# A mixture-of-streams attention block on one Trainium2 core: V computed batch by batch, with batch 1's input loaded among the V weights

## The chip, the cores and the metric

The kernel runs on one core of one Trainium2 chip. Time is device microseconds (us) of a run; a kernel's figure is the median of its runs. The profile is one execution, and its span is about 1.8 us shorter than the time of that run (119.9 of 121.67 for the kernel before). Each run carries the mean granted clock of TensorE, as a share of full speed. PE is TensorE and PEld its weight loads, DVE is VectorE, ACT is ScalarE, POOL is GpSimd; PSUM is the memory that takes PE's results. An evacuation is the copy of a finished sum out of PSUM by DVE or ACT. LN is layer norm.

## The reference, cut to what matters

There are two batches of 256 image tokens and 32 text tokens, width D = 1152, in bf16. The part at stake is the image side, up to the start of Q:

```python
mod_i = (_silu(c) @ wmod_img).reshape(B, 6, 1, D)        # shift, scale, gate
hi = _layernorm(x_img, axis=-1) * (1 + sci) + shi
qkvi = hi @ wqkv_img                                      # q, k, v
# ... the same for text; joint attention over 288 tokens; out_i = x_img + gai * (ai @ wo_img)
```

The kernel splits V: (LN(x)·(1+scale)) @ Wv comes first and needs no shift; the shift's share, one row per batch, is added later. So V can start when x and the scale weights are there, before the shift weights arrive.

## The kernel before

All weights come over one DMA queue in the order in which they are issued. These are the first loads (KT = 9 row groups of 128 rows, so V has 9 row groups of weights):

```python
for b in range(B):
    nc.sync.dma_start(x_i[:, b * TPB:(b + 1) * TPB, :], ...)        # both batches of x
SCC = (0, 3, 5, 7, K8, KT)
for r0, r1 in zip(SCC, SCC[1:]):
    nc.sync.dma_start(w_sc_i[:, r0:r1, :], sc_v[:, r0:r1, :])       # scale weights
for r0, r1 in ((0, 1), (1, 3), (3, 6), (6, KT)):
    nc.sync.dma_start(w_v_i[:, r0:r1, :], v_v[:, r0:r1, :])         # V weights
w_sh_i = load_w(2, wmod_img, 0)                                     # shift, then Q, K, ...
```

PE does every matmul and transpose in program order (`mm` and `tr` pin each instruction behind the one written before it; `pin` does so on DVE and ACT). PSUM is split into a main pool of six banks (`ps_mm`) and a small pool of two (`ps_tr`); a new tile takes a free bank of its pool or waits until one is released. Transposed x goes from PSUM to `xT_i`, and a DVE instruction scales it into `hS_i`, the operand of V that PE's weight loads take (PEld lines read `hS_i`).

```python
sc_cols(0, 3); warm_up(3); sc_cols(3, 5); warm_up(1); sc_cols(5, 7)   # (one line each)
x_transposes(0, 1)()                    # batch 1's transposes among the scale columns
out31 = x_transposes(3, 1)
sc_cols(7, K8); sc_cols(K8, KT)
out61 = x_transposes(6, 1)
out61()
# ... scale + 1, x_scale of both batches ...
v_open(A0, 0, 3)                        # A0: four tiles of batch 0, 512 wide
v_open(A1, 0, 3)                        # A1: two tiles of batch 1
v_open(A0 + A1, 3, KT - 2)
v_open(A0 + A1, KT - 2, KT, kt_major=False)
p_sh = mod_rows_of(w_sh_i, sT32)        # shift rows: need the shift weights
sh_i = mod_cols_of(p_sh, "shc")
v_open([(2, 1)], 0, 4)
# ... shift, the rest of V, the shift's share of V ...
qk_img(w_q_i, 0, ...)                   # the img Q block
```

## Time and profile before

The time is 121.91 us (121.82 to 122.08, 3 runs). The first lines of the page give the span and each engine's busy time:

```profile
span 119.9 us, 2608 instructions
PE 113.7 (95%) x1121; PEld 67.1 (56%) x1121; DVE 55.9 (47%) x146; ACT 34.4 (29%) x73; POOL 11.1 (9%) x28
```

PE is busy 95% of the span. This is the whole list of the view of waits on PE (who waited for whom: us in total, times, longest):

```profile
PE wps L61 <- DVE warm L121: 1.2, 1, 1.2
PE tp L64 <- DVE xn_i L187: 0.6, 1, 0.6
PE gps L61 <- DMA t<-in_wmod_img_dram: 0.5, 1, 0.5
PE vps L61 <- DVE hS_i L220: 0.3, 1, 0.3
```

Here `wps` are warm-up matmuls, `tp` transposes of x, `vps` sums of V, `gps` a pass that multiplies rows by the shift weights. The timeline of PE (start, length, instruction, idle before it) shows the stretch that the change touches:

```profile
14.24 11.90 PE L61 MATMUL vps<-t,hS_i 128*128 128x512 bf16 x54 [0.31 <-DVE hS_i L220]
26.61 1.29 PE L61 MATMUL gps<-t,sT 128*32 128x288 bf16 x36 [0.47 <-DMA t<-in_wmod_img_dram]
27.83 6.07 PE L61 MATMUL vps<-t,hS_i 128*128 128x512 bf16 x54
33.83 1.29 PE L61 MATMUL gps<-t,shT 128*32 128x288 bf16 x36
35.05 11.83 PE L61 MATMUL ps<-xT_i,t 128*128 128x512 bf16 x54
```

V starts at 14.24, PE waits 0.47 us for the shift weights at 26.61, and Q starts at 35.05. From 26.61 PE has no gap until the last output tile. So the start of Q, 35.05, is the number to watch: what moves it moves the end.

The trace also records when each transfer's sixteen parts have landed. The last part counts, because PE waits for the whole transfer:

| landed at, us | kernel before |
|---|---|
| V row groups 3 to 5 | 18.08 |
| shift weights | 26.57 |
| Q weights | 33.48 |

With 54 matmuls in 11.90 us (six per row group, about 1.3 us), PE reaches row group 3 at about 18.1, just as its rows land. The Q weights land at 33.5, so no reordering can start Q before that.

### The profile page before, as it was taken

To read this page: it belongs to the slowest core of one execution; us is meant where nothing else is said; L and a number is where in the kernel's file an instruction comes from. 1 tells how busy PE (TensorE), PEld (TensorE's weight loads), DVE (VectorE), ACT (ScalarE), POOL (GpSimd) and SP (SyncE) were. 2 spreads that over 40 slices of the span, in tenths; PEclk is the share of its full clock that TensorE was granted. 3 is DMA by queue.
4 is the path that set the end of the run, shared out by engine and by line. 5 is a ranking of instruction groups with operands and counts; after the bars stand their busy time and mean duration, and the time that the engine had idled before them with its cause. 6 is when DMAs were issued, how large, how long until landed. Compare 5 with 4: busy or idle time off the path is not lost.

```text
span 119.9 us, 2608 instructions
## 1 busy us (share of the span) xinstructions
PE 113.7 (95%) x1121; PEld 67.1 (56%) x1121; DVE 55.9 (47%) x146; ACT 34.4 (29%) x73; POOL 11.1 (9%) x28
## 2 busy tenths in 40 slices
PE   5989899989999999999999999999999999999980
PEld 2338744445664444544448448386777766567660
DVE  1568690066837222131721203037785756666670
ACT  4799700055713104101011111125348610000000
POOL 7410000000000000000000000000222708100000
PEclk9999999999999999999999999999999999999999
DMA  4999999999999999999999999999999991420222
GB/s 118 375 408 406 402 404 414 410 414 410 406 369 416 401 412 412 413 411 412 405 412 412 415 401 413 413 404 411 413 399 408 414 357 52 143 98 0 104 76 72
DMA packets 18502, 40.88 MB, mean 341 GB/s; under 512 B 907, under 2 KB 1435, under 8 KB 18491
## 3 DMA queue, kind: packets, MB, share of 16 engines
q1 hardware_dynamic: 17616, 39.56, 84.7%
q0 software_dynamic: 480, 0.89, 2.2%
q10 hardware_dynamic: 395, 0.26, 0.7%
q8 instruction: 9, 0.15, 0.4%
q14 instruction: 2, 0.02, 0.0%
HBM read 39.38 MB, written 1.34 MB: 340 GB/s over the span
## 4 chain that ended last, share of the span: by engine, by line
PE 74%; DMA 20%; SPq 1%; DVE 1%; issue 0%
PE ps L61 52%; DMA t<-in_wmod_img_dram 20%; PE gps L61 6%; PE aps L61 6%; PE vps L61 5%; PE sps L61 4%; PE pT_ps L64 1%; SPq L97 1%; DVE tmp L565 1%; DVE o L566 0%; SPq L101 0%; PE tpt L64 0%
## 5 line engine op out<-in xcount | busy, mean ns | idle before, releaser
L61 PE MATMUL ps<-xT_i,t 128*128 128x512 bf16 x162 | 36.0, 379 | 0.0
L61 PEld LDWEIGHTS <-t 128*128 128x128 bf16 x405 | 22.7, 97 | 19.3 <-issue 0.7
L61 PE MATMUL ps<-t,aT 128*128 128x384 bf16 (+3 forms) x153 | 20.2, 308 | 0.0
L61 PE MATMUL vps<-t,hS_i 128*128 128x512 bf16 (+1 forms) x108 | 18.0, 326 | 0.3 <-DVE hS_i L220 0.3
L61 PEld LDWEIGHTS <-aT 128*128 128x128 bf16 (+1 forms) x153 | 13.0, 101 | 7.1 <-issue 0.5
L61 PEld LDWEIGHTS <-hS_i 128*128 128x128 bf16 x108 | 9.0, 98 | 9.0 <-DVE hS_i L220 0.5
L155 DVE CAST qkT<-ps 128x512 bf16<-128x512 f32 (+1 forms) x6 | 3.8, 636 | 15.4 <-PE ps L61 15.4
L435 POOL DMA_DIRECT2D mod_scratch<-g_sb x4 | 2.5, 636 | 79.7 <-ACT g_sb L157 79.7
L565 DVE TENSOR_TENSOR tmp<-ps,gb 128x384 bf16<-128x384 f32 (+2 forms) x13 | 6.8, 527 | 6.3 <-PE ps L61 6.3
L61 PE MATMUL wps<-warm 128*128 128x512 bf16 x27 | 8.2, 454 | 1.2 <-DVE warm L121 1.2
L333 DVE TENSOR_SCALAR qkT<-ps 128x512 bf16<-128x512 f32 (+1 forms) x5 | 3.3, 665 | 10.8 <-PE ps L61 10.8
L335 ACT ACTIVATE qkT<-ps 128x512 bf16<-128x512 f32 (+1 forms) x6 | 3.3, 553 | 15.5 <-PE ps L61 15.5
L157 ACT CAST qkT<-ps 128x512 bf16<-128x512 f32 (+1 forms) x5 | 2.8, 565 | 16.6 <-PE ps L61 16.6
L155 DVE CAST v_i<-vps 128x512 bf16<-128x512 f32 x5 | 3.4, 689 | 8.0 <-PE vps L61 8.0
L61 PE MATMUL gps<-t,sT 128*32 128x288 bf16 x180 | 6.4, 287 | 0.5 <-DMA t<-in_wmod_img_dram 0.5
L61 PE MATMUL aps<-pT,v_i 128*128 128x288 bf16 x36 | 6.7, 287 | 0.0
L61 PEld LDWEIGHTS <-sT 128*32 128x32 bf16 x180 | 4.5, 96 | 2.4 <-issue 2.0
L537 DVE TENSOR_SCALAR aT<-aps,svc 128x288 bf16<-128x288 f32 x9 | 4.7, 518 | 2.4 <-PE aps L61 2.3
L61 PE MATMUL sps<-qkT 128*128 128x288 bf16 (+1 forms) x54 | 5.5, 287 | 0.0
L157 ACT CAST v_i<-vps 128x512 bf16<-128x512 f32 x4 | 2.3, 586 | 10.6 <-PE vps L61 10.6
L61 PEld LDWEIGHTS <-warm 128*128 128x128 bf16 x27 | 2.7, 110 | 4.6 <-issue 1.7
L539 ACT ACTIVATE aT<-aps,svc 128x288 bf16<-128x288 f32 x9 | 4.5, 501 | 2.5 <-PE aps L61 2.5
(94 smaller groups left out, 105.1 us busy)
## 6 DMA issues: line engine op xcount, KB each, us to landing
t<-in_wmod_txt_dram SPq DMA_DIRECT2D x3, 2592.0 KB, 18.7
t<-in_wqkv_txt_dram SPq DMA_DIRECT2D x3, 2592.0 KB, 15.5
t<-in_wmod_img_dram SPq DMA_DIRECT2D x2, 2592.0 KB, 18.8
t<-in_wqkv_img_dram SPq DMA_DIRECT2D x2, 2592.0 KB, 22.5
t<-in_wo_img_dram SPq DMA_DIRECT2D x1, 2592.0 KB, 17.7
t<-in_wo_txt_dram SPq DMA_DIRECT2D x1, 2592.0 KB
t<-in_wqkv_img_dram SPq DMA_DIRECT2D x2, 864.0 KB, 11.9
x_i<-in_x_img_dram SPq DMA_DIRECT2D x2, 576.0 KB, 4.4
```

The lines of the kernel that those rows point to most:

```text
L61: return pin(nc.tensor.matmul(*a, **k))
L64: return pin(nc.tensor.transpose(*a, **k))
L97: nc.sync.dma_start(x_i[:, b * TPB:(b + 1) * TPB, :], x_img[b].rearrange("(p t) d -> p t d", t=TPB))
L155: nc.vector.tensor_copy(out_ap, in_ap)
L157: nc.scalar.copy(out_ap, in_ap)
L333: nc.vector.tensor_scalar_mul(out_ap, in_ap, SCALE)
L335: nc.scalar.mul(out_ap, in_ap, SCALE)
L435: nc.gpsimd.dma_start(gsc[si, b, :].rearrange("(g j) -> g j", g=NGG), g_sb[b:P:32, :])
L537: nc.vector.tensor_scalar(dst, aps[:], bias, None, op0=ALU.add)
L539: nc.scalar.activation(dst, aps[:], ACT.Identity, bias=bias)
L565: nc.vector.tensor_mul(tmp[:, 0:n], ps[:, 0:n], gb[:, b, c0:c0 + n])
```

## The change

Its intent is to start V sooner and to keep DMA-fed work ahead of PE. Only batch 0's x comes ahead of the scale weights; V of batch 0 is computed alone, in five banks (four tiles of 512 columns, the two 128-wide ends share one); batch 1's x lands among the V rows, and its layer norm and transposes are to run beneath V of batch 0.

```diff
-    for b in range(B):
+    def load_x(b):
         nc.sync.dma_start(x_i[:, b * TPB:(b + 1) * TPB, :], ...)
 ...
+    load_x(0)
+    load_rows(w_sc_i, sc_v, 0, 3, 5, 7, K8, KT)
+    load_rows(w_v_i, v_v, 0, 1, 3)
+    load_x(1)
+    load_rows(w_v_i, v_v, 3, 6, KT)
 ...
-    sc_ps = ps_mm.tile([P, KT, B], f32, tag="mm")
+    sc_ps = ps_tr.tile([P, KT, B], f32, tag="tr")
 ...
-        tr_pool = b == 0 and k0 < 6
+        tr_pool = k0 == 0
 ...
+    for out in [x_transposes(k0, 0) for k0 in (0, 3, 6)]:
+        out()
+    sc_cols(0, 3)
+    warm_up(3)
+    sc_cols(3, 5)
+    warm_up(2)
+    sc_cols(5, 7)
+    warm_up(1)
+    sc_cols(7, KT)
+    pin(nc.vector.tensor_scalar_add(sc1_i[:], sc_ps[:], 1.0))
+    x_scale(0, KT, 0)
     s2 = ln_sums(x_i[:, 2, :], xn_i[:, 2, :])          # LN of batch 1 ...
 ...
+    v_block(0, 0, 7)
+    outs = [x_transposes(k0, 1) for k0 in (0, 3, 6)]
+    for n, out in enumerate(outs):
+        out()
+        x_scale(3 * n, 3 * n + 3, 1)
+    v_block(0, 7, KT, kt_major=False)
 ...
+    v_block(1, 0, KT, kt_major=False, hooks={(2 * TPB - 1, 1): img_shift})
```

The shift rows now come late in V (`img_shift`). The separate `v_last` goes, and V has ten evacuations instead of nine.

More of the change, by code (lines that the diff above doesn't have):

```diff
@@ L95, with load_rows @@
     sc_v, v_v = wview(wmod_img, D), wview(wqkv_img, 2 * D)
-    for b in range(B):
+    def load_x(b):
         nc.sync.dma_start(x_i[:, b * TPB:(b + 1) * TPB, :], x_img[b].rearrange("(p t) d -> p t d", t=TPB))
-    SCC = (0, 3, 5, 7, K8, KT)
-    for r0, r1 in zip(SCC, SCC[1:]):
-        nc.sync.dma_start(w_sc_i[:, r0:r1, :], sc_v[:, r0:r1, :])
-    for r0, r1 in ((0, 1), (1, 3), (3, 6), (6, KT)):
-        nc.sync.dma_start(w_v_i[:, r0:r1, :], v_v[:, r0:r1, :])
+    def load_rows(t, sv, *cuts):
+        for r0, r1 in zip(cuts, cuts[1:]):
+            nc.sync.dma_start(t[:, r0:r1, :], sv[:, r0:r1, :])
+    load_x(0)
[3 more added lines that the diff above has]
+    load_rows(w_v_i, v_v, 3, 6, KT)
     w_sh_i = load_w(2, wmod_img, 0)
@@ L213, in copy_out @@
         def copy_out():
-            pin(nc.scalar.copy(dst, tp[:]) if b == 0 or k0 == 6 else nc.vector.tensor_copy(dst, tp[:]))
+            pin(nc.vector.tensor_copy(dst, tp[:]) if k0 == 3 else nc.scalar.copy(dst, tp[:]))
         return copy_out
@@ L225, with v_block @@
     accs = {}
-    def v_open(ids, k0, k1, kt_major=True):
-        for key in ids:
-            if key not in accs:
-                accs[key] = ps_mm.tile([P, VW], f32, tag="mm", name="vps")
-        loop = [(kt, key) for kt in range(k0, k1) for key in ids] if kt_major else \
-            [(kt, key) for key in ids for kt in range(k0, k1)]
-        for kt, (i, cc) in loop:
-            mm(accs[(i, cc)][:], lhsT=hS_i[:, kt, i * P:(i + 1) * P], rhs=w_v_i[:, kt, cc * VW:(cc + 1) * VW],
-               start=(kt == 0), stop=(kt == KT - 1), skip_group_check=True)
-            if kt == KT - 1:
+    def v_block(b, k0, k1, kt_major=True, hooks={}):
+        tiles = range(b * TPB, (b + 1) * TPB)
+        keys = [(i, cc) for cc in range(2) for i in tiles] + [(i, 2) for i in tiles]
+        for i, cc in keys:
+            if (i, cc) not in accs:
+                accs[(i, cc)] = accs[(i - 1, 2)] if cc == 2 and i % TPB else \
+                    ps_mm.tile([P, VW], f32, tag="mm", name="vps")
+        loop = [(kt, key) for kt in range(k0, k1) for key in keys] if kt_major else \
+            [(kt, key) for key in keys for kt in range(k0, k1)]
+        for kt, (i, cc) in loop:
+            if kt == k0 and (i, cc) in hooks:
+                hooks[(i, cc)]()
+            t = i % TPB
+            o, n = (t * P, P) if cc == 2 else (0, VW)
+            mm(accs[(i, cc)][:, o:o + n], lhsT=hS_i[:, kt, i * P:(i + 1) * P], rhs=w_v_i[:, kt, cc * VW:cc * VW + n],
+               start=(kt == 0 and (cc < 2 or t == 0)), stop=(kt == KT - 1), skip_group_check=True)
+            if kt == KT - 1 and cc < 2:
                 evac(v_i[:, i, cc * VW:(cc + 1) * VW], accs[(i, cc)][:])
-    A0 = [(0, 0), (1, 0), (0, 1), (1, 1)]
-    A1 = [(2, 0), (3, 0)]
+            elif kt == KT - 1 and t == TPB - 1:
+                evac(v_i[:, b * TPB:(b + 1) * TPB, 2 * VW:D],
+                     accs[(i, cc)][:, 0:TPB * P].rearrange("p (t n) -> p t n", t=TPB))
     def ln_norm_dve(i, mv):
@@ L258 @@
     ln_norm(x_i[:, 2, :], s2[:, 0:1], r2, P, xn_i[:, 2, :])
-    x_transposes(0, 0)()
-    x_transposes(3, 0)()
-    x_transposes(6, 0)()
-    sc_cols(0, 3)
-    warm_up(3)
-    sc_cols(3, 5)
-    warm_up(1)
-    sc_cols(5, 7)
-    x_transposes(0, 1)()
-    out31 = x_transposes(3, 1)
-    sc_cols(7, K8)
-    sc_cols(K8, KT)
-    out61 = x_transposes(6, 1)
-    out61()
-    pin(nc.vector.tensor_scalar_add(sc1_i[:], sc_ps[:], 1.0))
-    x_scale(0, 3, 0)
-    x_scale(0, 3, 1)
-    out31()
-    for b in range(B):
-        x_scale(3, 6, b)
-    for b in range(B):
-        x_scale(6, KT, b)
-    v_open(A0, 0, 3)
-    v_open(A1, 0, 3)
-    v_open(A0 + A1, 3, KT - 2)
-    v_open(A0 + A1, KT - 2, KT, kt_major=False)
+    v_block(0, 0, 7)
[4 more added lines that the diff above has]
+    v_block(0, 7, KT, kt_major=False)
     NGG = 4
@@ L303, in mod_cols_of, with img_shift @@
         return t
-    p_sh = mod_rows_of(w_sh_i, sT32)
-    sh_i = mod_cols_of(p_sh, "shc")
-    v_open([(2, 1)], 0, 4)
-    nc.vector.tensor_copy(shT32[:, :, 0:B], sh_i[:, :, 0:B])
     hT_i = xT_i
-    for kt in range(KT):
-        for b in range(B):
-            h = hT_i[:, kt, b * NI:(b + 1) * NI]
-            if b == 0 or kt % 3 == 0:
-                nc.vector.tensor_scalar(h, h, sc1_i[:, kt, b:b + 1], sh_i[:, kt, b:b + 1],
-                                        op0=ALU.mult, op1=ALU.add)
-            else:
-                nc.scalar.activation(h, h, ACT.Identity, bias=sh_i[:, kt, b:b + 1], scale=sc1_i[:, kt, b:b + 1])
-    pin(nc.scalar.dma_start(x_t[:], xt_flat[:, :]))
-    v_open([(2, 1)], 4, KT)
-    v_open([(3, 1)], 0, KT)
-    def v_last():
-        vps = ps_mm.tile([P, NIT, P], f32, tag="mm")
-        for i in range(NIT):
-            for kt in range(KT):
-                mm(vps[:, i, :], lhsT=hS_i[:, kt, i * P:(i + 1) * P], rhs=w_v_i[:, kt, 2 * VW:D],
-                   start=(kt == 0), stop=(kt == KT - 1))
-        evac(v_i[:, :, 2 * VW:D], vps[:])
+    def img_shift():
+        sh_i = mod_cols_of(mod_rows_of(w_sh_i, sT32), "shc")
+        nc.vector.tensor_copy(shT32[:, :, 0:B], sh_i[:, :, 0:B])
+        for kt in range(KT):
+            for b in range(B):
+                h = hT_i[:, kt, b * NI:(b + 1) * NI]
+                if b == 0 or kt % 3 == 0:
+                    nc.vector.tensor_scalar(h, h, sc1_i[:, kt, b:b + 1], sh_i[:, kt, b:b + 1],
+                                            op0=ALU.mult, op1=ALU.add)
+                else:
+                    nc.scalar.activation(h, h, ACT.Identity, bias=sh_i[:, kt, b:b + 1], scale=sc1_i[:, kt, b:b + 1])
+        pin(nc.scalar.dma_start(x_t[:], xt_flat[:, :]))
+    v_block(1, 0, KT, kt_major=False, hooks={(2 * TPB - 1, 1): img_shift})
     def qk_evac(out_ap, in_ap, blk):
@@ L454, in txt_gate @@
                                     gsc[1, b, :].rearrange("(r g j) -> g r j", r=2, g=2)[g].partition_broadcast(NT))
-    v_last()
     shift_v_rows()
```

## The prediction

> **What bounds the kernel now.** TensorE: the page gives PE 113.7 us busy of 119.9 (95%). In the chain of waits one DMA wait matters: the img shift weights land at 26.57; PE, done at 26.14, waits 0.47 us. From 26.61 PE runs without a gap to about 115.8. So the time is decided by when PE starts the img Q block, 35.05 in the timeline. V starts at 14.24. DMA moves about 405 to 412 GB/s until 97 us; by the landing records: x0 4.7, x1 6.1, scale rows 8.2 to 12.7, V rows 13.7 / 15.2 / 18.1 / 20.1, shift 26.6, Q weights 33.5. Reordering can win at most 35.05 - 33.5 = 1.5 us: faster by over 2% is practically excluded.
>
> **What the change does, costed.**
>
> 1. Start of V. The scale rows land 1.4 us earlier, but PE was not waiting for them: its order is warm-up matmuls (0.22 us each), transposes (12 in 0.66) and scale columns (18 in 0.46). The change takes 0.66 of transposes out of this stretch and adds two warm-ups (0.43): V starts near 14.0, 0.24 earlier.
>
> 2. V rows. Before, six 512-wide matmuls per row group (0.216 each, 1.30 per group) reach group 3 at 18.13, just as its rows land (18.08). Now batch 0 has four of 512 and two of 128 (0.059 each, from the chain's 54 in 6.00 us): 0.98 per group. It reaches group 3 at 16.95, and the rows still land near 18.1, because the same bytes precede them. New PE wait: 1.1 us, which swallows the earlier start. Group 7 ends near 22.0.
>
> 3. Batch 1's transposes (18 in 1.0 us) lay among the scale columns before V; now they follow inside V.
>
> 4. Banks. Batch 0 holds five of the main pool's six banks, its sums still open. Batch 1's first transpose tile goes to the other pool, its second takes the only spare bank, its third needs that same bank. It must wait for: transposes (0.49), ScalarE copy of tile one (0.80), three VectorE scalings queued ahead (0.67), VectorE copy of tile two (0.55), handovers: from 22.0 to about 24.65, while PE runs out of work at 22.66. New PE gap: about 2.0 us.
>
> Then groups 7 and 8 (1.96) to 27.0; batch 1, 36 x 0.216 + 18 x 0.059 = 8.8; two shift-row passes of 1.22. Q starts near 38.2 instead of 35.05. The 0.47 wait disappears (included). All of it is on the critical path: +3.1 us.
>
> LN of batch 1 (x1 lands near 15.2, normalized near 19.3) is hidden. [...] the page here shows a full clock over its shorter gaps, so I expect none.
>
> **Prediction:** 125.0 us, range 123.0 to 125.9. Faster by over 2%: 0.01; within 2%: 0.29; slower by over 2%: 0.70.
>
> **What would show it.** PE waiting about 1.1 us at vps for V rows near 17 to 18; about 2 us before batch 1's last transposes, released by VectorE's copy of xT_i; no wait at the shift rows; Q starting near 38; clock full; PE unbroken afterwards.
>
> **What would make it wrong.** If the third transpose tile finds a free bank, the 2.0 us gap goes: about 123.1. If V rows land earlier, the first wait shrinks by as much. Later stages could change, since evacuations swap engines (ten in V instead of nine).

## The result, and the profile after

The changed kernel takes 125.56 us (125.4 to 125.89, 4 runs) against 122.0 (121.82 to 122.24, 4 runs). The ratio is 1.0294 (95% interval 1.0266 to 1.0323): slower. A ratio here comes from the fast runs of both kernels in the same rounds and lies close to the ratio of their mean times, so it is not quite the ratio of the medians quoted.

The page's first lines, then PE's waits:

```profile
span 123.6 us, 2603 instructions
PE 114.5 (93%) x1113; PEld 67.6 (55%) x1123; DVE 55.7 (45%) x146; ACT 34.6 (28%) x74; POOL 11.1 (9%) x28
```

```profile
PE tp L64 <- DVE xT_i L218: 1.7, 1, 1.7
PE wps L61 <- DVE warm L125: 1.2, 1, 1.2
PE vps L61 <- DMA t<-in_wqkv_img_dram: 1.0, 1, 1.0
PE vps L61 <- DVE hS_i L224: 0.7, 1, 0.7
PE aps L61 <- DVE pT L516: 0.4, 1, 0.4
```

Three waits are new: transposes for a DVE copy of `xT_i` (1.7), V for its weight rows (1.0), and, much later, attention for `pT` (0.4). The wait for the shift weights is gone. (The wait for the first scaled x, `hS_i`, grew from 0.3 to 0.7; it lies before V starts and is contained in that start.) The timeline shows the first two in place (lines of PE, and those of ACT and DVE between the two transposes):

```profile
14.15 3.10 PE L61 MATMUL vps<-t,hS_i 128*128 128x512 bf16 x17 [0.67 <-DVE hS_i L224]
...
18.20 4.06 PE L61 MATMUL vps<-t,hS_i 128*128 128x512 bf16 x24 [0.95 <-DMA t<-in_wqkv_img_dram]
...
18.56 0.57 DVE L191 TENSOR_SCALAR xn_i<-x_i,sm,rstd 128x1152 bf16<-128x1152 bf16 x1
...
22.10 0.83 PE L64 MATMUL tp<-ident,xn_i 128*128 128x128 bf16 x12
22.63 0.80 ACT L218 COPY xT_i<-tp 128x768 bf16<-128x768 bf16 x1 [4.18 <-PE tp L64]
23.46 0.68 DVE L224 TENSOR_SCALAR hS_i<-xT_i,sc_i 128x256 bf16<-128x256 bf16 x3 [4.33 <-ACT xT_i L218]
...
24.06 0.55 DVE L218 COPY xT_i<-tp 128x768 bf16<-128x768 bf16 x1
...
24.66 0.49 PE L64 MATMUL tp<-ident,xn_i 128*128 128x128 bf16 x6 [1.73 <-DVE xT_i L218]
...
25.21 7.72 PE L61 MATMUL vps<-t,hS_i 128*128 128x512 bf16 x38
...
38.35 1.90 PE L61 MATMUL ps<-xT_i,t 128*128 128x512 bf16 x8
```

Batch 0's three row groups take PE only 3.1 us, so it stands at row group 3 until 18.20, just after the rows land (18.16), while DMA keeps moving 396 to 412 GB/s (from 14 to 20 us). Batch 1's normalised x is ready at 19.1 (18.56 + 0.57), long before it is used. Then twelve transposes run, and the last six wait through a chain: ACT copies tile one, DVE scales it, DVE copies tile two, and only then is the bank of tile two free for tile three. Q starts at 38.35 instead of 35.05, 3.30 us later.

The sum of what can be read off: V starts 0.09 earlier (-0.09); V rows +0.95; shift weights -0.47; bank +1.73; the 18 transposes that now stand inside V, 12 in 0.66 and 6 in 0.33, +1.0. That is 3.12 of the 3.30; the other 0.2 is handovers that I have not separated.

The span grew by 3.7, so another 0.4 came after Q started. The chain of waits of the changed kernel has this near its end (start, length, what), where `pT`, DVE's copy of the transposed attention weights for PE, is late:

```profile
89.67 0.36 DVE g_sb L159
90.03 0.38 DVE nmx L467
...
92.05 0.52 DVE pT L516
92.57 0.05 issue
92.62 2.01 PE aps L61 x15
```

`g_sb` is the evacuation of a gate row. Evacuations of this kind alternate between DVE and ACT by a counter, and with ten in V instead of nine every later one changed engine. In the kernel before, this copy was on ACT; now it sits on DVE ahead of a softmax maximum (`nmx`). That is a suspicion at this point.

### The profile page after: what moved, and what is told of

It is laid out like the page before. It is cut to its first block, busy times and chain, and to the rows that moved or that the text cites. A ratio compares the mean times of both kernels' runs of the same rounds, so it can differ in the third digit from the quotient of the medians.

```text
span 123.6 us, 2603 instructions
## 1 busy us (share of the span) xinstructions
PE 114.5 (93%) x1113; PEld 67.6 (55%) x1123; DVE 55.7 (45%) x146; ACT 34.6 (28%) x74; POOL 11.1 (9%) x28
## 4 chain that ended last, share of the span: by engine, by line
PE 73%; DMA 14%; DVE 6%; ACT 3%; issue 1%; SPq 0%; ACTq 0%
PE ps L61 50%; PE vps L61 12%; DMA t<-in_wqkv_img_dram 9%; PE aps L61 6%; DMA t<-in_wmod_img_dram 4%; PE gps L61 4%; ACT e L470 1%; DVE nmx L467 1%; DVE pb L474 1%; PE tp L64 1%; ACT xT_i L218 1%; DVE hS_i L224 1%; DVE pb L476 1%; DVE rs L472 1%; DVE tmp L558 1%
## 5 line engine op out<-in xcount | busy, mean ns | idle before, releaser
L61 PE MATMUL wps<-warm 128*128 128x512 bf16 x28 | 9.4, 488 | 1.3 <-DVE warm L125 1.2
L327 DVE TENSOR_SCALAR qkT<-ps 128x512 bf16<-128x512 f32 (+1 forms) x6 | 3.8, 636 | 13.2 <-PE ps L61 13.2
L159 DVE CAST qkT<-ps 128x512 bf16<-128x512 f32 (+1 forms) x5 | 3.3, 663 | 11.5 <-PE ps L61 11.5
L224 DVE TENSOR_SCALAR hS_i<-xT_i,sc_i 128x256 bf16<-128x256 bf16 x18 | 3.9, 282 | 4.5 <-ACT xT_i L218 4.3
L218 ACT COPY xT_i<-tp 128x768 bf16<-128x768 bf16 x4 | 3.1, 800 | 7.6 <-PE tp L64 7.6
L61 PE MATMUL aps<-pT,v_t 128*128 128x288 bf16 x18 | 5.1, 286 | 0.0
```

The source lines that it names most:

```text
L61: return pin(nc.tensor.matmul(*a, **k))
L159: nc.vector.tensor_copy(out_ap, in_ap)
L218: pin(nc.vector.tensor_copy(dst, tp[:]) if k0 == 3 else nc.scalar.copy(dst, tp[:]))
L224: pin(nc.vector.tensor_scalar(hS_i[:, kt, b * NI:(b + 1) * NI], xT_i[:, kt, b * NI:(b + 1) * NI], sc1_i[:, kt, b:b + 1], None, op0=ALU.mult))
L327: nc.vector.tensor_scalar_mul(out_ap, in_ap, SCALE)
```

## The experiments

Each was run for five rounds beside the kernel before on the same chip; twelve kernels in three sets. Results were correct in all. Sets were on different occasions, so ratios to the kernel before are what to compare between sets.

### a_bank: a free bank for the third transpose tile

```diff
-        tr_pool = k0 == 0
+        tr_pool = k0 == 0 or (b == 1 and k0 == 6)
```

> The changed kernel with one edit: batch 1's third transpose tile goes to the small pool, whose two banks are free then, instead of waiting for the main pool's one spare bank. Theory (the bank costs 1.7 us): PE's wait for VectorE's copy of xT_i (1.73 us in the changed kernel's profile) disappears, transposes run as one block of about 1.0 us from about 22.1, Q starts near 36.7 instead of 38.4, and the time is about 123.8 instead of 125.56. Rival (the gap is the lateness of batch 1's x and its LN, the bank only happens to end it last): PE still waits there or just after, at hS_i of batch 1, for over 1 us, and the time stays above 125.0.

It took 123.64 us, ratio 1.0142 (1.012 to 1.0164), against 1.0294. The wait for `xT_i` is gone from PE's list, and all 18 transposes run in one piece:

```profile
18.51 4.06 PE L61 MATMUL vps<-t,hS_i 128*128 128x512 bf16 x24 [1.63 <-DMA t<-in_wqkv_img_dram]
22.41 1.17 PE L64 MATMUL tp<-ident,xn_i 128*128 128x128 bf16 x18
23.42 7.94 PE L61 MATMUL vps<-t,hS_i 128*128 128x512 bf16 x39
```

The bank theory holds and the rival, late x, falls: batch 1's x arrives even later here (landed at 16.37, against 15.04 in the changed kernel) and PE does not wait for it. In this execution V began at 13.79, earlier than in the changed kernel's, and its rows landed at 18.47, later than there: the 0.36 of an earlier start and the 0.31 of later rows both went into a longer wait (1.63). An earlier start of V buys nothing while the rows decide.

### a_vcut: V rows in finer transfers

```diff
-    load_rows(w_v_i, v_v, 3, 6, KT)
+    load_rows(w_v_i, v_v, 3, 4, 6, KT)
```

> The changed kernel with one edit: V rows 3 to 5 arrive as two transfers (row 3, rows 4 and 5) instead of one. Theory (PE's 0.95 us wait for V rows is for a transfer of three row groups of which it needs only the first): the row 3 transfer lands near 16.3 and the wait falls to below 0.2 us; group 7 ends about 0.9 earlier, Q starts near 37.5, time about 124.7. Rival (the byte order alone decides: PE is ahead of DMA whatever the cut, so the wait moves to rows 4 and 5 landing at 18.1): a wait of 0.5 us or more shows at the second part, and the time stays above 125.1. Second rival: PE comes earlier but batch 1's normalised x (done at 19.1) or the bank takes it back: the gap before the transposes grows by as much.

It took 124.4 us, ratio 1.0214 (1.0198 to 1.0231): 0.8% off, and the interval lies clear of the changed kernel's. The bytes and their order are the same, yet the wait nearly vanishes:

```profile
PE tp L64 <- DVE xT_i L218: 1.7, 1, 1.7
...
PE vps L61 <- DMA t<-in_wqkv_img_dram: 0.2, 1, 0.2
```

Row group 3 alone landed at 16.58 in this execution, groups 4 and 5 at 17.97. So PE had been waiting for rows that it did not need yet. The prediction's reason, that the same bytes precede the rows, was right about the landing of the whole transfer and not the last word on the wait. The bank gap neither grew nor shrank, so both rivals fall.

### a_x1late: batch 1's x behind V rows 3 to 5

```diff
-    load_x(1)
-    load_rows(w_v_i, v_v, 3, 6, KT)
+    load_rows(w_v_i, v_v, 3, 6)
+    load_x(1)
+    load_rows(w_v_i, v_v, 6, KT)
```

> The changed kernel with one edit: batch 1's x is loaded after V rows 3 to 5 instead of before them. Theory: V rows 3 to 5 land 1.4 us earlier, so the 0.95 us wait goes, but x of batch 1 lands near 18.2 and its LN takes 4.1 us as before, to 22.3, so PE, done with group 7 at about 21.1, waits about 1.2 us for the normalised x ahead of the transposes; the bank gap of 1.7 stays; time 125.3 to 125.8, no gain. Rival (the place of x1 among the V rows is the fault, as the change's loss began with it): 124.6 or less.

It took 125.67 us, ratio 1.0304 (1.027 to 1.0339): no gain, as the theory had it. The wait changed its name:

```profile
PE tp L64 <- DVE xT_i L219: 1.7, 1, 1.7
...
PE tp L64 <- DVE xn_i L192: 0.9, 1, 0.9
...
PE vps L61 <- DMA t<-in_wqkv_img_dram: 0.4, 1, 0.4
```

Now the transposes wait for the normalised x (0.9) and V waits for rows 6 to 8 (0.4). The wait for x was 0.9, not 1.2, and the 0.4 for rows 6 to 8 was not foreseen; the sum was as expected. Swapping two transfers that are both needed soon only renames the wait.

### a_swap and b_swap: the evacuation counter

a_swap adds one line to the changed kernel after V; b_swap adds the same line to the kernel before, after `v_last()`.

```diff
+    evac_idx[0] += 1
```

> The changed kernel with one edit: the counter that alternates evacuations between VectorE and ScalarE is advanced by one after V, so that from Q on every evacuation is on the engine that it had in the kernel before. Theory (the last 0.4 us of the loss come from the swap: in the changed kernel the gate row's copy sits on VectorE ahead of a softmax maximum, and the copy of pT comes 0.43 late for PE): the wait of PE for pT disappears, the V stage is as in the changed kernel (Q near 38.4), time about 125.15. Rival (it comes from the late x_txt or the late weights): the wait of 0.43 stays and the time is 125.5.

> The kernel before with one edit: the same counter advanced by one after V, so that from Q on each evacuation is on the other engine. Theory (the swap alone costs 0.4): PE waits about 0.4 us for VectorE's copy of pT, and the time is about 122.4 instead of 122.0. Rival (the swap does nothing without the later start of Q): no wait at pT, time 122.0.

a_swap took 125.2 us, ratio 1.028 (1.0257 to 1.0303); that interval overlaps the changed kernel's, so the time alone proves nothing. Its profile does: the wait for `pT` is gone. (Its execution waited 1.27 for V rows, 0.3 more than the changed kernel's, which hides most of the gain in the span.) The distance from Q's start to the end of the span says the same over all profiles: 85.2 to 85.3 us in the five kernels with swapped engines (changed kernel, a_bank, a_vcut, a_x1late, b_swap), 84.7 to 84.9 in all others but b_shift, whose profile is a slow one. b_swap took 122.38 us, ratio 1.0045 (1.0023 to 1.0067), and its list of waits has the line that the kernel before lacks:

```profile
PE vps L61 <- DVE hS_i L220: 1.4, 2, 1.1
...
PE aps L61 <- DVE pT L524: 0.4, 1, 0.4
```

So the swap alone costs about 0.4 us in either kernel, and the late Q is not needed for it. That it is the gate row's copy, among all that changed engine, rests on the chain above alone. The first line is a lesson in reading. The named DVE scaling had ended long before; the V rows 1 and 2 of that execution landed at 16.47 instead of 15.15, and PE resumed at 16.51. A wait for several things is put down to one of them; where that one had long been done, it was another, here a DMA. This was the slowest of the six runs (122.88).

### a_three: the three edits together

> The changed kernel with the three edits a_bank, a_vcut and a_swap together. Theory (three separate costs that add): by the ratios 1.0294, 1.0142, 1.0214 and 1.028, the losses taken away are 1.5, 0.8 and 0.1 to 0.35%, so about 1.003 of the kernel before, 122.1 to 122.3 us; no wait at the bank, at pT, and at most 0.2 at V rows; Q starts near 35.3. Rival (they overlap: taking one away uncovers another wait, such as batch 1's scaled x): 1.010 or more, with a new wait in the V stage.

It took 122.59 us, a little above the 122.1 to 122.3 expected, ratio 1.0045 (1.0006 to 1.0084). Taking 1.52, 0.80 and 0.14% off 1.0294 leaves 1.0048, so the result agrees with three costs that add; the rival's 1.010 lies outside the interval. None of the three waits is in its profile, but for the V rows this profile cannot tell, since PE ran at half clock just while they landed (below). What is left against the kernel before is near the 0.5 us that the transposes inside V (+1.0) and the vanished shift wait (-0.47) leave; this remainder is worked out, not tested. Q started at 36.84 in the profiled execution, not at 35.3, for a reason that none of the theories had. It was the slowest of six (123.42), and in the page's row of PE's granted clock one slice of 3 us reads 5. The view by windows narrows it down (window, PE busy, ..., granted clock, DMA share, GB/s):

```profile
PEclk9999959999999999999999999999999999999998
```

```profile
13.00:14.00 1.00, 0.33 (x13) 0.25 (x11) 0.56 (x3) 0.00 (x0) 0.00 (x0) 1.00 1.03 424
14.00:15.00 1.00, 1.00 (x4) 0.41 (x5) 1.00 (x7) 0.00 (x0) 0.00 (x0) 0.80 1.02 397
15.00:16.00 1.00, 1.00 (x5) 0.52 (x4) 1.00 (x5) 0.95 (x1) 0.00 (x0) 0.50 1.03 394
...
18.00:19.00 1.00, 1.00 (x7) 0.50 (x6) 0.95 (x2) 0.40 (x3) 0.00 (x0) 0.99 1.04 410
```

The clock was halved from about 14.6 to 18.0, some 3.4 us, with PE at 1.00 busy. The timeline of PE just before it:

```profile
12.04 0.59 PE L61 MATMUL sc_ps<-sT,t 128*128 128x2 bf16 x18
12.49 0.38 PE L61 MATMUL wps<-warm 128*128 128x512 bf16 x1
12.70 0.59 PE L61 MATMUL sc_ps<-sT,t 128*128 128x2 bf16 x18
13.96 8.68 PE L61 MATMUL vps<-t,hS_i 128*128 128x512 bf16 x42 [0.67 <-DVE hS_i L224]
```

So the 3.4 us before the dip (from 11.2) held two-column matmuls (`sc_ps`), three warm-ups, an idle 0.67 us and the first matmuls of V, but no transpose: those of batch 0 had ended at 10.0.

### a_best, a_best2 and a_warm: an attempt to beat both, and its clock

a_best joins a_bank and a_swap with a better order of loads, batch 1's transposes one row group later, the copy of tile two ahead of the scalings, and two warm-up matmuls among the scale columns instead of six:

```diff
-    load_rows(w_v_i, v_v, 0, 1, 3)
+    load_rows(w_v_i, v_v, 0, 1, 3, 4, 5)
     load_x(1)
-    load_rows(w_v_i, v_v, 3, 6, KT)
+    load_rows(w_v_i, v_v, 5, 6, 7, KT)
 ...
-    warm_up(3)
+    warm_up(1)
     sc_cols(3, 5)
-    warm_up(2)
-    sc_cols(5, 7)
     warm_up(1)
+    sc_cols(5, 7)
 ...                       # v_block(0, 0, 8); all three copies; x_scale(0, KT, 1); v_block(0, 8, KT)
```

> An attempt to beat both from the changed kernel: a_bank and a_swap, with V rows 3 and 4 ahead of batch 1's x and rows 5, 6 and 7 to 8 behind it, two warm-up matmuls among the scale columns instead of six, batch 1's transposes one group later and VectorE's copy of the second tile ahead of all nine scalings. Theory: V starts near 12.9 to 13.0 instead of 14.15, no wait over 0.3 us in the V stage, Q near 34.3 to 34.6 against 35.05 in the kernel before: 121.0 to 121.4 us. Rival: the clock falls without the warm-ups, or a wait for rows or for batch 1's scaled x takes it back: 122 or more.

It took 122.52 us, ratio 1.0019 (0.9971 to 1.0067): it does not beat the kernel before. V started at 12.80, as hoped, but Q at 35.08, not at 34.3 to 34.6, even at full clock: PE waited 0.42 for rows and 0.20 for the normalised x inside V (the first above the 0.3 that was expected at most), and V now also contains the 18 transposes (1.0); the time saved at the start went there. In three of its six runs the mean clock was 0.986 (one of them counted as slow). That is not all of its median: another run took 123.13 at a clock of 0.999. Two further runs test the clock: a_best2 is the same kernel again, and a_warm has the six warm-ups back.

> a_best again, unchanged, on the same chip as a_warm. Theory: again a part of the runs, about half, at a mean clock near 0.986 and about 0.9 us longer, the others near 121.6. Rival: all runs at 1.0 and near 121.6, so that the dips of the first time were that chip's.

> a_best with the six warm-up matmuls among the scale columns put back (3, 2 and 1, as in the changed kernel). In a_best the runs of mean clock 0.986 were near 122.5, those of 1.0 near 121.6; 0.986 is what one window of 3.4 us at half clock gives over 120 us (worked out: 1 - 0.5 x 3.4 / 120). Theory (the missing warm-ups let the clock fall in some runs): V starts near 13.7, Q near 35.4 to 35.6, median about 122.0 to 122.2, and fewer runs at 0.986 than in a_best2. Rival (the dips are the chip's and come as often with the warm-ups): as many runs at 0.98 to 0.99 as in a_best2.

| same chip, same rounds | median, us | ratio (95%) | mean clock of its six runs |
|---|---|---|---|
| a_best2 (two warm-ups) | 122.0 | 1.0017 (0.9972 to 1.0061) | 0.986, 1.0, 0.986, 1.0, 0.986, 0.98 |
| a_warm (six warm-ups) | 121.8 | 0.9992 (0.9953 to 1.0032) | 0.995 to 0.998 |

In time the two cannot be told apart, as their intervals overlap; a_warm missed its own marks a little, with V at 14.11 (13.7 expected), Q at 35.31 (35.4 to 35.6) and a median of 121.8 (122.0 to 122.2). The clocks do differ. In the profile of a_best2 the page shows the dip in V's first slices. PE was busy for 2.92 of the 3 us from 9 to 12 us, then idle for 0.67 us until V started at 12.86; the clock fell at 12.69:

```profile
PEclk9999689999999999999999999999999999999999
```

```profile
9.00:12.00 3.00, 2.92 (x94) 1.00 1.03 396
12.00:14.00 2.00, 1.12 (x10) 0.67 1.06 415
14.00:15.00 1.00, 1.00 (x5) 0.50 1.05 422
```

With six warm-ups no run of six dipped, with two four of six did (seven of twelve over both sets). The Trainium skill, TensorE: Matmul & The Clock Gate, Part 1, describes a monitor that lets PE's clock run at full or at half rate, by PE's activity in free-running windows of 3413 ns, and Part 4 that transposes do not count as busy in the same way. The dip's 3.4 us and its 0.50 agree, and so do the trace's clock records: those of a_three last 10.24, 3.41 and 102.40 us, multiples of 3413 ns. The 3.4 us before a_best2's dip (9.3 to 12.7) hold the last five transposes, 81 matmuls of two columns, one warm-up and most of the idle 0.67 us. Whether a window falls badly on such a stretch differs from run to run, as a free-running window would have it. Transposes are not needed for it, as a_three shows, and how they count, no run here shows; whether the two-column matmuls or the idle 0.67 us weigh more, no run here separates. Six warm-ups are not a guarantee either: of all runs with six (the changed kernel and its variants, 36 runs) three show 0.981 to 0.985, one each of a_three, a_swap and a_x1late, and one run of the kernel before shows 0.986.

a_warm with full clock is level with the kernel before: the changed order can be mended, but not made better, by what I tried.

### b_shift, b_shift2 and b_two: the one wait of the kernel before

b_shift moves 0.86 us of V work ahead of the shift rows in the kernel before; b_shift2 repeats it, since three of b_shift's six runs, the profiled one (136.07) among them, fell in the slow state; b_two also cuts the V rows finer.

```diff
-    p_sh = mod_rows_of(w_sh_i, sT32)
-    sh_i = mod_cols_of(p_sh, "shc")
     v_open([(2, 1)], 0, 4)
+    p_sh = mod_rows_of(w_sh_i, sT32)
+    sh_i = mod_cols_of(p_sh, "shc")
 # b_two in addition:
-    for r0, r1 in ((0, 1), (1, 3), (3, 6), (6, KT)):
+    for r0, r1 in ((0, 1), (1, 2), (2, 3), (3, 4), (4, 6), (6, KT)):
```

> The kernel before with one edit: the four half-sums of the next V tile (0.86 us of PE work) run ahead of the shift rows instead of behind them. Theory (the shift weights' arrival at 26.57 costs PE 0.47 us and nothing else): the wait goes, Q starts near 34.6, time about 121.35. Rival (DMA paces the Q weights or the start of VectorE's modulation then paces Q): unchanged, 121.8, with a new wait at Q.

> b_shift again, unchanged, as three of its runs fell in the slow state. Theory: 0.996 of the kernel before, near 121.4, faster by 0.3 to 0.5 us in every quiet run, with no wait of PE for the shift weights and Q near 34.6. Rival: 0.999 to 1.001.

> b_shift with the V rows cut finer (row groups 1 and 2 apart, 3 apart from 4 and 5). In the kernel before, PE reaches row group 3 at 18.13 and its transfer lands at 18.1 to 18.5, and in one profile (b_swap) rows 1 and 2 landed at 16.5, a wait of 1.1 us. Theory: PE no longer depends on the last engine of a large transfer, so the median is 0 to 0.2 us below b_shift2 and the spread of its runs is smaller. Rival: more transfers cost issue time or bandwidth and it is 0.2 us or more slower.

| kernel | median of all runs, us | ratio of fast runs (95%) |
|---|---|---|
| b_shift | 122.44 (fast runs 121.41, 121.48, 121.53) | 0.9953 (0.9911 to 0.9995) |
| b_shift2 | 121.75 | 0.997 (0.993 to 1.0011) |
| b_two | 121.31 | 0.9953 (0.9915 to 0.9991) |

In b_shift2 the wait is gone and Q starts at 34.64, which is what the removal of 0.47 should give:

```profile
27.06 1.29 PE L61 MATMUL gps<-t,sT 128*32 128x288 bf16 x36
...
34.64 3.63 PE L61 MATMUL ps<-xT_i,t 128*128 128x512 bf16 x15
```

The theory stands by the profile; in time it is at the edge of what the intervals resolve, and the repeat alone would leave it unclear: three of its five fast runs were within 0.1 us of the kernel before (121.8), not 0.3 to 0.5 faster as expected. b_two has the lowest median, about 0.5% below the kernel before. It is 0.44 below b_shift2, where 0 to 0.2 was expected, its fast runs spread no less (0.77 against 0.50), and its profile still waits for V rows, those of group 2:

```profile
PE vps L61 <- DMA t<-in_wqkv_img_dram: 0.3, 1, 0.3
```

So its theory, that PE no longer depends on late parts, is not shown. Whether the finer cut adds anything to b_shift the intervals do not tell (both ratios are 0.9953).

## Why the prediction was right

- **Time.** Predicted 125.0 (123.0 to 125.9), measured 125.56.
- **PE bounds, and Q's start is the measure.** Right: 3.30 of the span's growth of 3.7 us is the later Q (predicted 3.1). The steps on the way were right too, so this is not errors that cancel: V rows 18.1 predicted and PE back at 18.20, last transposes 24.65 and 24.66, Q 38.2 and 38.35.
- **Nothing to gain from the earlier scale weights.** V started 0.09 earlier instead of 0.24 (between 13.72 and 14.15 over the profiles with that warm-up order). Right in kind; a_bank shows that an earlier start only lengthens the wait for rows.
- **V rows.** Predicted 1.1, measured 0.95; a_vcut brings it down to 0.19. The prediction gave the bytes ahead of the rows as the cause. Part of it is the size of the transfer: group 3 had arrived 1.4 us before groups 4 and 5 when it could be told apart.
- **Banks.** Predicted 2.0, measured 1.73, released by the copy that was named; a_bank takes it away. Most of the difference is in the counting: the profile calls the twelve transposes before the gap 0.83 long, the prediction 0.66.
- **LN of batch 1 hidden; clock full.** Both right for the changed kernel ("I expect none" means no loss of clock). The clock argument looked at idle time alone, though, and a_best2 shows that this isn't enough: the clock halved with no gap over 0.7 us after the first transposes.
- **Mis-sized term: "PE unbroken afterwards".** PE waited 0.43 us for `pT`. The prediction named the swap of engines as something that could change later stages, but put no number on it; it measured 0.4 us, in both kernels (a_swap, b_swap). It accounts for most of the 0.56 us by which the time exceeded the prediction.

## What to carry to other kernels

When work is split so that an engine consumes its data faster, compare the new rate with the landing times of each transfer, and cut transfers to what the next step needs: the same bytes in the same order cost 1 us less. Count the banks that are open when a second consumer starts, and follow the chain that frees the next one; here a free bank stood idle in the other pool. And if evacuations alternate by a counter, one evacuation more or less shifts all later ones to the other engine, far from the edit.

## What the Trainium skill lacked or had wrong

- TensorE: Matmul & The Clock Gate, "Why this matters for your kernels", warns of idle gaps over about 3 us. Here the clock halved for 3.4 us though PE had no gap over 0.7 us from 9 us on (2.92 of 3.00 us busy at 9 to 12 us in a_best2). The page says of transposes that they count differently (Part 4), but not that the clock can fall after a stretch of mostly two-column matmuls without any, as in a_three, nor how many full matmuls keep it: with two among the scale columns seven of twelve runs dipped, with six three of 36.
- DMA: Bandwidth & Descriptors, "Latency and other measured facts", puts slow engines (7 and 15) down to software DMA, as a best guess. Here transfers of the hardware queue end late as well, and the trace has no packet of the software queue before 94 us: of the sixteen parts of V rows 3 to 5, half had landed at 16.70 and the last at 18.16 in the changed kernel. Which engine is late, no view here shows. Cutting does not remove this lag (in a_vcut half of row 3's parts had landed at 15.30, the last at 16.58); it only lets row 3 land ahead of rows 4 and 5 (17.97).
- PSUM — Partial Sum Buffer, Specifications (TRN2): eight banks agree with this kernel's pools of six and two. No page tells what a bank held by an open sum costs when transposes need it; here it was 1.73 us.
